# A linear-attention and Fourier-FFN kernel on one core: a form of its own for the first batch, and another plan

## The chip, the core and the metric

The kernel runs on 1 core of one Trainium2 chip. The metric is the time of one execution on the device in microseconds (us), the median of several runs; lower is better. TensorE (PE in the profile, PEld its weight loads) does the matmuls, VectorE (DVE), ScalarE (ACT) and GpSimd (POOL) the element-wise work, and DMA transfers are issued here from SyncE's queue (SP), some from ACT's and POOL's.

## The reference

```python
def _attn_ref(q, k, v, g_norm):                  # (8, 8, 576, 64) each, g_norm (64,)
    kv = np.einsum('bhsd,bhse->bhde', k, v)
    out = np.einsum('bhsd,bhde->bhse', q, kv)
    rms = np.sqrt(np.mean(out * out, axis=-1, keepdims=True) + 1e-06)
    return (out / rms * g_norm).astype(np.float32)

def _moe_ref(x, w_ch1, w_ch2):                   # x (8, 576, 512), w_ch1 (512, 2048), w_ch2 (2048, 512)
    X = np.fft.fft(x, axis=1)
    X = np.fft.fft(X, axis=2)
    u = x + np.real(X).astype(np.float32)
    mu = np.mean(u, axis=-1, keepdims=True)
    var = np.mean((u - mu) ** 2, axis=-1, keepdims=True)
    un = (u - mu) / np.sqrt(var + 1e-06)
    return (u + np.maximum(un @ w_ch1, 0.0) @ w_ch2).astype(np.float32)
```

Between the two, the attention's output is laid out as x with its 8 heads side by side (512 wide).

## The kernel before

**Stages of a batch.** Each of 8 batches passes through these steps. The k-v sums (`plan_kv`, L509): four pairs of heads, ten matmuls each, into one state kvt. The turns of q (`plan_q`, L557): a batch's 576 rows are loaded as two sides of 288, each as three classes of 96 rows (row index modulo 3), and every class of a side is transposed by four transposes, copied to fq by ACT. The attention output (`plan_out`, L582), one unit of 16 matmuls for each class t, with both sides; ACT copies it to x and squares it, DVE sums the squares (L606), POOL multiplies x by g (L617). When all three classes of a batch are summed, `plan_y` makes one scale factor for all of them (L635 to L651, ACT, POOL and DVE in turn). `plan_fold` multiplies x by it (L679), folds the two sides and the two halves of the columns (L690, then POOL's even and odd parts, L697) and splits the result into a high and a low part xh and xl (L703, L706). The sequence transform (`plan_seq`, L721) is four groups of nine matmuls, three for each class; its result is split again (L734, L738). The column transform (`plan_chn`, L755) takes six groups of six; ACT, DVE and POOL add its result to x (L767, L775, L785, L788). x is stored as u and transposed (`plan_turn`, L842) into unT, high and low (L851, L854).

**The FFN.** Per block of 512 tokens, `plan_first` (ps_h, L366) multiplies by a slice of w_ch1, 12 matmuls of 512 columns, then ReLU and split (L375, L378); `plan_second` and `plan_early` (acc, L383) multiply by the slice of w_ch2. Both use three matmuls where one would do at lower precision (high by high, high by low, low by high). The normalisation is moved behind: w_ch1's slices have their column means taken out, and a row's scale is applied at the end. A weight slice is prepared in `plan_w`: a load (raw), an ACT pass (L299), five DVE steps (L306 to L316), a sum (L896), for w_ch1 a sum over its rows (L321), a matmul with 1/512 that spreads it (ps_w, L329) and a subtraction (L333), then high and low part (L908, L913). Three slices of each are ready early (the ring wA).

**What sets the order.** Every instruction is an `Op` with an engine, a cost, a rank and what it depends on. `Plan.run` walks through time with these costs and gives each engine, whenever it is free, the ready op of lowest rank; what it emits is the engines' final order. Buffers come from rings with a fixed number each (RINGS: eight PSUM banks "p8", six k and v pieces "kv", four "fq", and so on). Rank is 10 times the batch plus a stage, FILL and more for the FFN. Where TensorE would be free, it emits filler: two matmuls of 512 columns on `still`, into a bank ps_s that nobody reads (L438). A filler op has the highest rank of all and may start from 12 us of planned time on (`SPARE_FROM`). On an engine, instructions run in that order and each waits for its semaphores. At most eight DMA transfers of the SP and ACT queues are under way: the ninth waits for the first.

## Time and profile before

| | us |
|---|---|
| median of 3 runs (lowest, highest) | 1032.32 (1023.65, 1032.94) |
| profiled execution: its own time | 1028.71 |
| profiled execution: span | 1026.9 |
| TensorE busy (98% of the span) | 1004.7 |
| DVE, ACT, POOL busy | 482.5, 328.4, 321.7 |
| mean granted clock of TensorE | 0.994 |

The page gives busy time and share of the span for each engine, the span in 40 slices, the DMA queues, the chain that ended last (89% of it on TensorE), and the costliest groups of instructions. A row of the timeline has the start in us, the duration, the engine, the line, the operation with output and inputs, how many instructions are merged in it, and in brackets how long the engine stood idle before and what ended that. A row of the windows has the stretch, its length, then busy time and number of instructions for PE, PEld, DVE, ACT and POOL, the granted clock, the share of time in which DMA engines were busy, and GB/s. A plain fp32 matmul appears as two records, a transpose or a matmul of the split kind as one. Durations of matmuls in a row overlap: a row's last one drains while the next row begins.

### The profile page before, as it was taken

What the parts mean: (1) busy time and instruction counts of PE and PEld (TensorE: products, weight loads), DVE (VectorE), ACT (ScalarE), POOL (GpSimd) and SP (SyncE); (2) the same over time, 40 slices, a digit from 0 to 9 for tenths busy, and PEclk for the clock granted to TensorE, in tenths of its full rate; (3) what the DMA queues carried; (4) which work ended last, traced back from release to release, by engine and by line L of the source; (5) the groups of instructions that cost most, each with busy time, mean ns of one, the idle gap of its engine ahead of it and who ended that gap; (6) DMA issues with size and microseconds to landing.
All of it is one profiled execution on the core that took longest, in us unless ns stands there. A gap on an engine that the chain in (4) does not pass through costs nothing.

```text
span 1026.9 us, 15221 instructions
## 1 busy us (share of the span) xinstructions
PE 1004.7 (98%) x5988; PEld 844.2 (82%) x5988; DVE 482.5 (47%) x839; ACT 328.4 (32%) x655; POOL 321.7 (31%) x332
## 2 busy tenths in 40 slices
PE   5999999999999999999999999999999999999998
PEld 4788899788888878888788888888888888888886
DVE  3778675446678657999932313131221221221312
ACT  2556665546544433343222121121021021121110
POOL 0466876655856110223253132301020020020010
PEclk9899999999999999999999999999999999999999
DMA  9998785863337653668171615230220400500201
GB/s 236 234 214 221 183 255 168 220 188 132 128 126 240 262 185 128 241 209 300 46 246 31 215 37 210 68 137 21 105 90 20 174 22 1 184 21 1 103 0 41
DMA packets 109771, 144.92 MB, mean 141 GB/s; under 512 B 51854, under 2 KB 76482, under 8 KB 104580
## 3 DMA queue, kind: packets, MB, share of 16 engines
q1 hardware_dynamic: 100980, 127.04, 39.8%
q10 hardware_dynamic: 6800, 10.62, 2.9%
q0 software_dynamic: 1920, 6.29, 2.2%
q8 instruction: 47, 0.77, 0.3%
q14 instruction: 24, 0.20, 0.1%
HBM read 92.52 MB, written 51.40 MB: 140 GB/s over the span
## 4 chain that ended last, share of the span: by engine, by line
PE 89%; DMA 3%; DVE 3%; ACT 1%; SPq 1%; issue 1%; POOL 1%; ACTq 0%; DVEq 0%; POOLq 0%
PE ps_h L366 36%; PE acc L383 36%; PE ps_f L721 3%; PE ps_f L755 3%; PE ps_o L582 3%; PE ps_k L509 2%; PE ps_s L438 2%; PE ps_t L842 1%; PE ps_q L557 1%; DMA vm<-in_v_dram 1%; DMA draw<-in_dft_s_dram 1%; DMA part_scr<-part 1%; PE ps_w L329 0%; ACT x L597 0%; DMA u_scr<-x 0%
## 5 line engine op out<-in xcount | busy, mean ns | idle before, releaser
L383 PE MATMUL acc<-w,hh 128*128 128x512 f32 x1152 | 357.5, 391 | 0.0
L366 PE MATMUL ps_h<-unTh,w 128*128 128x512 f32 x1152 | 356.0, 390 | 0.3 <-DVE pm L775 0.3
L378 DVE SCALAR_TENSOR_TENSOR hl<-ps_h,hh 128x512 fp32r<-128x512 f32 x144 | 99.3, 689 | 375.9 <-ACT hh L375 375.8
L366 PEld LDWEIGHTS ps_h<-unTh,w 128*128 128x128 f32 x1152 | 215.2, 188 | 44.7 <-PE ps_h L366 0.7
L383 PEld LDWEIGHTS acc<-w,hh 128*128 128x128 f32 x1152 | 214.0, 188 | 43.6
L375 ACT ACTIVATE hh<-ps_h 128x512 fp32r<-128x512 f32 x144 | 86.1, 598 | 474.8 <-PE ps_h L366 474.6
L383 PE MATMUL acc<-w,hl 128*128 128x512 f32 x576 | 224.6, 390 | 0.5 <-DVE hl L378 0.4
L366 PE MATMUL ps_h<-unTl,w 128*128 128x512 f32 x576 | 224.2, 389 | 0.0
L1194 POOL TENSOR_TENSOR uu<-uu,up 128x512 f32<-128x512 f32 x36 | 45.8, 1296 | 308.7 <-ACT up L1186 307.4
L383 PEld LDWEIGHTS acc<-w,hl 128*128 128x128 f32 x576 | 108.1, 188 | 23.9 <-DVE hl L378 1.3
L366 PEld LDWEIGHTS ps_h<-unTl,w 128*128 128x128 f32 x576 | 108.1, 188 | 22.6
L617 POOL TENSOR_TENSOR x<-x,gb 96x512 f32<-96x512 f32 (+1 forms) x48 | 63.4, 1337 | 56.6 <-ACT x L597 54.9
L606 DVE TENSOR_REDUCE ss<-ps_o 96x8 f32<-96x512 f32 (+1 forms) x48 | 32.9, 687 | 44.9 <-ACT ps_o L602 36.1
L913 POOL TENSOR_TENSOR w<-wap,w 128x512 fp32r<-128x512 f32 x18 | 23.3, 1293 | 96.5 <-ACT w L908 93.2
L1239 DVE SCALAR_TENSOR_TENSOR uu<-acc,rs_yb,uu 128x512 f32<-128x512 f32 x36 | 25.2, 744 | 40.6 <-PE acc L383 40.6
L697 POOL TENSOR_TENSOR xe<-ab 96x256 f32<-96x256 f32 (+1 forms) x48 | 36.7, 789 | 19.9 <-DVE ab L690 19.8
L1136 POOL TENSOR_TENSOR up<-up 128x512 f32<-128x512 f32 x16 | 20.5, 1291 | 69.2 <-DMA up<-next_scr 69.1
L721 PE MATMUL ps_f<-cs,xh 96*128 96x290 f32 (+1 forms) x192 | 40.5, 306 | 0.0
L582 PEld LDWEIGHTS ps_o<-kvt,fq 64*96 64x96 f32 (+1 forms) x768 | 34.6, 162 | 5.7 <-issue 4.2
L597 ACT COPY x<-ps_o 96x512 f32<-96x512 f32 (+1 forms) x48 | 28.1, 585 | 33.0 <-PE ps_o L582 26.4
L582 PE MATMUL ps_o<-kvt,fq 64*96 64x64 f32 (+1 forms) x768 | 37.8, 248 | 0.0
L854 DVE TENSOR_TENSOR unTl<-ps_t,unTh 128x384 fp32r<-128x384 f32 (+13 forms) x80 | 33.5, 476 | 7.9 <-ACT unTh L851 7.5
(106 smaller groups left out, 1043.2 us busy)
## 6 DMA issues: line engine op xcount, KB each, us to landing
raw<-in_moe_w_ch_dram SPq DMA_DIRECT2D x32, 512.0 KB
unTh<-unT_scr SPq DMA_DIRECT2D x11, 1024.0 KB
unTl<-unT_scr SPq DMA_DIRECT2D x11, 1024.0 KB
qt<-in_q_dram SPq DMA_DIRECT2D x16, 576.0 KB
unT_scr<-unTh SPq DMA_DIRECT2D x9, 1024.0 KB
unT_scr<-unTl SPq DMA_DIRECT2D x9, 1024.0 KB
part_scr<-part ACTq DMA_DIRECT2D x36, 256.0 KB
up<-part_scr SPq DMA_DIRECT2D x36, 256.0 KB
```

What stands on the lines that cost most here:

```text
L366: nc.tensor.matmul(ps, w[c][:, kc * P : (kc + 1) * P], unT[a][:, kc, :], start=(kc == 0 and n == 0), stop=(kc == KC - 1 and n == 2),)
L375: nc.scalar.activation(hh, ps, AF.Relu)
L378: nc.vector.scalar_tensor_tensor(hl, ps, 0.0, hh.bitcast(F32), ALU.max, ALU.subtract)
L383: nc.tensor.matmul(acc, hpair[a][:, i * P : (i + 1) * P], w[c], start=(first and n == 0), stop=(last and n == 2),)
L582: nc.tensor.matmul(pss[s].t[:n, at : at + D], fqs[side].t[half, m, :n], kvt.t[half, m], start=True, stop=True,)
L606: nc.vector.tensor_reduce(ss.t[0][:n, :, t, s::2], pss[s].t[:n].rearrange("p (u m e) -> p u m e", u=2, e=D), AX.X, ALU.add,)
L617: nc.gpsimd.tensor_tensor(v_, v_, gb[:n].unsqueeze(1).to_broadcast([n, H, D]), ALU.mult)
L697: nc.gpsimd.tensor_tensor(o[:, s], a[:, 0], a[:, 1], ALU.subtract if s else ALU.add)
L721: nc.tensor.matmul(ps.t[:, :NS], xs[t].t[a][:n, part, ch * P : (ch + 1) * P], cs[:n, part, c, t, :], start=(idx == 0), stop=(idx == 8),)
L755: nc.tensor.matmul(ps.t[:n, :ND], pt.t[a][:, part, ch, offs[t] : offs[t] + n], cd[:, part, c, ch, :], start=(idx == 0), stop=(idx == 5),)
L854: nc.vector.tensor_tensor(unTs[j].t[1][:, :, to], view()[:, :, lo:hi], unTs[j].t[0][:, :, to].bitcast(F32), ALU.subtract,)
L1194: lambda i=i: nc.gpsimd.tensor_tensor(us_[i].t, us_[i].t, parts[i].t, ALU.add),
```

## The change

It has four parts.

1. **The plan.** It first runs the first batch's ops alone (`first`, set by `mark`), notes when each starts (`aim`), and then runs all ops, in which another op may not start on an engine (or on the port that DVE and POOL share) if it would reach into the next aim by more than `SLIP`. Costs of loads are changed, TensorE's ops cost twice as much until 6.6 us of planned time, and as long as the FFN has not begun, filler goes ahead of later batches' work when TensorE's columns in the last 3414 ns are fewer than 3400. Filler may start at once. 84 filler matmuls are emitted instead of 122.
2. **Queries of batches 0 and 1** are loaded in pieces of three rows (768 bytes) instead of one row (256 bytes). A class of a head then lies apart in the tile, so `plan_q` turns it by eight plain matmuls with the identity, 64 columns of weights each, instead of four transposes.
3. **The first batch's output** (`plan_first_out`). The state is kept twice, kvt and kvg = kvt times g, and each class's output is computed with both. The first is squared and summed only, the second multiplied by the class's own scale factor straight from PSUM into x. No copy, no product with g, and no scale factor for all classes. Classes go in the order 2, 1, 0, the sequence transform is issued class by class (three matmuls to each group), and two classes' column transforms are added by DVE instead of POOL.
4. **Weights.** The first slices of w_ch1 and w_ch2 are loaded ahead of k on SP, the mean of the three early w_ch1 slices is taken by four matmuls on TensorE without the sum over rows, and their low half is made by POOL instead of DVE. The last k and v pair of batch 0 has buffers of its own.

```diff
-SPARE = 120
-SPARE_FROM = 12000
+SPARE = 200
+SPARE_FROM = 0
...
+    def w_mean4(ps, af):
+        for c in range(KC):
+            nc.tensor.matmul(
+                ps[:, :P], mean_t, af[:, c * P : (c + 1) * P], start=(c == 0), stop=(c == KC - 1)
+            )
...
+                if b == 0 and pr == NPAIR - 1:
+                    main = Buf("h", lambda c=c: h_tile(c + "h").bitcast(F32).rearrange(
+                        "p (h j d) -> p h j d", h=2, j=4
+                    ))
...
+        kvg = Buf("h", lambda: h_tile("kvg").rearrange("p (c d) -> p c d", d=D))
+        scaled = op(
+            "DVE", 330, rank(b, KV),
+            lambda: nc.vector.tensor_tensor(
+                kvg.t[:, :NPAIR].bitcast(F32), ps.t[:, : NPAIR * D].rearrange("p (c d) -> p c d", d=D),
+                gb.unsqueeze(1).to_broadcast([P, NPAIR, D]), ALU.mult,
+            ),
+            mm + [i_gb], [ps, kvg],
+        )
...
+            if wide:
+                nc.sync.dma_start(
+                    qt.t[:TR].rearrange("p (h e) -> p h e", h=H), src.rearrange("h (p j) d -> p h (j d)", j=3)
+                )
...
+                if wide:
+                    for s in range(2):
+                        at = ((2 * m + s) * 3 + j) * D
+                        nc.tensor.matmul(
+                            view()[s * D : (s + 1) * D, m, :], qt.t[:n, at : at + D], ident[:n, :n],
+                            start=True, stop=True,
+                        )
...
+    def plan_first_out(b, t, fqs, done, kvt, kvg, x, sq):
...
+        a = op("PE", 1500, r, lambda: mm(0), done, [kvt, sq] + pss[0] + fqs)
+        g = op("PE", 1500, r + 0.5, lambda: mm(1), done, [kvg, x] + pss[1] + fqs)
...
+            c = op("ACT", 594, r - D1, square, [a], [pss[0][s]])
+            reds.append(op("DVE", 684, r - D1, red, [c], [pss[0][s], sq]))
...
+        c = op("ACT", 300, r - D1, root, reds, [sq])
+        d = op("DVE", 80, r - D1, mean, reds, [sq])
+        d = op("DVE", 800, r - D1, inverse, [c, d], [sq, pss[0][0]])
...
+            ms.append(op("DVE", 690, r - D1, mul, [g, d], [pss[1][s], sq, x]))
...
-        a = op("PE", 1200, r, mm, dones + [dft["s", part]], [ps, pt] + xs)
+        if b == 0:
+            a = []
+            for t in (2, 1, 0):
+                a = [op(
+                    "PE", 400, r, lambda t=t: mm_of(t), a + [dones[t], dft["s", part]] + gate_seq,
+                    [ps, pt, xs[t]],
+                )]
...
+        quick = b == 0 and t < 2
...
+        if quick:
+            adds = [op("DVE", 720, r, lambda s=s: add_q(s), pms, [x] + pss) for s in range(2)]
...
+        early = ring_ == "wA"
+        away = slow or early and which == 1
...
-            eng = nc.gpsimd if slow else nc.vector
+            eng = nc.gpsimd if away else nc.vector
...
-                    plan_w(which, f, "wA", lambda: wA, rank(0, FOLD) + f, [], (0, 3, 11)[f])
+                    plan_w(which, f, "wA", lambda: wA, 9 + f / 10, [], (-1, 6, 9)[f])
```

**The order, at three places.** TensorE at the start of the program, before (ps_k is the k-v sums, ps_q the turns of q, ps_w the mean of a weight slice, ps_s filler):

```order
L509 MATMUL ps_k<-vm,km 64x64 x8
L509 MATMUL ps_k<-vr,kr 64x64 x2
L438 MATMUL ps_s<-still 128x512 x16
L557 MATMUL ps_q<-ident,qt 128x97 x4
L557 MATMUL ps_q<-ident,qt 128x96 x8
L329 MATMUL ps_w<-wp,mean_t 128x128
```

and after, from its first matmul to the first attention output (ps_o):

```order
L507 MATMUL ps_s<-still 128x512 x28
L393 MATMUL ps_w<-wa,mean_t 128x128 x4
L590 MATMUL ps_k<-vm,km 64x64 x8
L590 MATMUL ps_k<-vr,kr 64x64 x2
L590 MATMUL ps_k<-vh,kh 64x64 x8
L507 MATMUL ps_s<-still 128x512 x4
L660 MATMUL ps_q<-ident,qt 64x97 x8
L660 MATMUL ps_q<-ident,qt 64x96 x24
L507 MATMUL ps_s<-still 128x512 x8
L747 MATMUL ps_o<-kvt,fq 96x64 x16
L747 MATMUL ps_o<-kvg,fq 96x64 x16
```

28 filler matmuls and the first slice's mean now stand ahead of the k-v sums, and the 16 filler among the k-v sums are gone.

SP's queue at the start, before (km and kr are pieces of k, raw a weight slice, qt a side of q; gb is g, sgn_t a table of signs):

```order
L488 DMA km<-in_k_dram 128x2x256
L497 DMA kr<-in_k_dram 64x8x64
L488 DMA km<-in_k_dram 128x2x256 x2
L296 DMA raw<-in_moe_w_ch_dram 128x4x256
L296 DMA raw<-in_moe_w_ch_dram 128x1024
L424 DMA gb<-in_g_norm_dram 128x64
L532 DMA qt<-in_q_dram 96x24x64
L538 DMA qt<-in_q_dram 1x8x64
L423 DMA sgn_t<-in_sign_dram 128x18
```

and after:

```order
L493 DMA gb<-in_g_norm_dram 128x64
L359 DMA raw<-in_moe_w_ch_dram 128x4x256
L359 DMA raw<-in_moe_w_ch_dram 128x1024
L569 DMA km<-in_k_dram 128x2x256
L578 DMA kr<-in_k_dram 64x8x64
L569 DMA km<-in_k_dram 128x2x256 x2
L569 DMA kh<-in_k_dram 128x2x256
L629 DMA qt<-in_q_dram 96x8x192
L639 DMA qt<-in_q_dram 1x8x64
```

g and the two weight slices moved ahead of k; the last k piece (kh) no longer waits for a buffer of the ring, and q's rows are three times as long.

DVE around the first batch's scale factor, before (ss the sums of squares, cs and cd the transforms' tables, ab the folded result, ps_y the scale factor):

```order
L606 TENSOR_REDUCE ss<-ps_o 97x2x4 x2
L606 TENSOR_REDUCE ss<-ps_o 96x2x4
L462 TENSOR_TENSOR cd<-draw,cd 128x516 x2
L642 RECIPROCAL rs_y<-rs_s 97x48
L306 TENSOR_SCALAR ps_a<-ps_a 128x512
L651 TENSOR_TENSOR ps_y<-rs_y,rs_s 97x48
L679 TENSOR_TENSOR x<-x,ps_y 97x512 x2
L690 TENSOR_TENSOR ab<-x 97x512
```

and after, the first of the three classes:

```order
L536 TENSOR_TENSOR cs<-draw,cs 97x870 x2
L764 TENSOR_REDUCE ss<-ps_o 96x2x4 x2
L776 TENSOR_SCALAR m<-ss 96x2x8
L536 TENSOR_TENSOR cd<-draw,cd 128x516
L781 RECIPROCAL ps_o<-rs_s 96x16
L782 TENSOR_TENSOR ss<-ps_o,m 96x2x8
L783 SCALAR_TENSOR_TENSOR ss<-ss,ps_o 96x2x8
L784 SCALAR_TENSOR_TENSOR rs_s<-ss,ps_o 96x2x8
L792 TENSOR_TENSOR x<-ps_o,rs_s 96x8x64 x2
L870 TENSOR_TENSOR ab<-x 96x512
```

A class's inverse, products and fold now follow its own two sums; five of a weight slice's steps no longer stand between the reciprocal and the scale factor.

More of the change, by code (lines that the diff above doesn't have):

```diff
@@ L106, in run @@
[L106 to L126 removed]
+    def run(self):
+        first = [o for o in self.ops if o.first]
+        if first:
+            self.go(first, False)
+        for o in first:
+            o.aim = o.start
+        return self.go(self.ops, True)
@@ L443, with mark @@
     dft = {}
+    EARLY = 2
+    def mark(since):
+        for o in plan.ops[since:]:
+            o.first = True
     def plan_dft(part, dst, src, n, r, key):
@@ L673, in plan_fold @@
         r = rank(b, FOLD)
-        ms = []
-        for s in range(2):
+        given, ms = ms, list(ms or [])
+        for s in range(0 if given else 2):
             def mul(s=s):
@@ L898, in plan_w @@
             mean = bank_buf("ps_w")
-            if slow and not late_:
+            if early:
+                pass
+            elif slow and not late_:
                 e = op("POOL", 1400, r, lambda: w_sum_pool(af_(), pf_()[:, :P]), [e], held)
@@ L916, in plan_w @@
         w_done[which, f] = op(
-            "POOL" if slow else "DVE", 1291 if slow else 689, r, lo, [g], src + [tile_],
+            "POOL" if away else "DVE", 1291 if away else 689, r, lo, [g], src + [tile_],
             port=(which == 1),
```

337 lines of the change are left out of this document (241 added, 96 removed).

## Prediction

> **What bounds the kernel now.** I read the busy times first, then windows by stage, then the front row by row (start, duration, what; in brackets the idle time ahead and what ended it).
>
> ```profile
> PE 1004.7 (98%) x5988; PEld 844.2 (82%) x5988; DVE 482.5 (47%) x839; ACT 328.4 (32%) x655; POOL 321.7 (31%) x332
> L438 PE MATMUL ps_s<-still 128*128 128x512 f32 x122 | 35.3, 434 | 0.1
> 0.00:20.00 20.00, 9.58 (x78) 7.57 (x80) 5.75 (x11) 2.12 (x3) 0.90 (x8) 1.00 1.00 225
> 20.00:69.00 49.00, 46.49 (x523) 38.27 (x524) 33.63 (x47) 29.73 (x61) 24.27 (x27) 0.93 1.11 241
> 69.00:100.00 31.00, 30.29 (x379) 26.56 (x378) 27.68 (x51) 18.41 (x44) 17.91 (x21) 1.00 0.74 191
> ```
>
> TensorE is busy for 98% of the span, and from 69 us on it hardly waits: 30.29 of 31 us. Its order is fixed by the plan. So the time is the work in that order, plus the filler (ps_s, L438, whose results nobody reads), plus TensorE's waits, plus what a lowered clock adds. Only the last three can be saved, and they lie in the front: in the first 20 us TensorE is busy for 9.58 us, 5.0 of them filler.
>
> ```profile
> 1.34 0.31 DVE L430 CAST still<-ident 128x128 fp32r<-128x128 f32 x1 [0.28 <-POOL ident masks.py:199]
> 4.90 1.12 PE L509 MATMUL ps_k<-vm,km 128*64 128x64 f32 x16 [4.90 <-DMA vm<-in_v_dram]
> 8.66 0.48 PE L509 MATMUL ps_k<-vr,kr 64*64 64x64 f32 x4 [2.64 <-DMA vr<-in_v_dram]
> 9.97 1.12 PE L509 MATMUL ps_k<-vm,km 128*64 128x64 f32 x16 [0.84 <-DMA vm<-in_v_dram]
> 12.90 5.00 PE L438 MATMUL ps_s<-still 128*128 128x512 f32 x16
> 19.93 0.69 PE L509 MATMUL ps_k<-vm,km 128*64 128x64 f32 x16 [2.04 <-DMA km<-in_k_dram]
> 36.20 0.33 PE L509 MATMUL ps_k<-vr,kr 64*64 64x64 f32 x4 [1.53 <-DMA vr<-in_v_dram]
> 38.15 0.69 PE L509 MATMUL ps_k<-vm,km 128*64 128x64 f32 x16 [0.74 <-DMA vm<-in_v_dram]
> 41.30 2.16 PE L557 MATMUL ps_q<-ident,qt 97*128 97x97 f32 x12 [0.24 <-DVE cd L462]
> 43.16 3.38 PE L438 MATMUL ps_s<-still 128*128 128x512 f32 x8
> 65.25 5.21 PE ps_s L438 x22
> 70.47 4.81 PE ps_f L721 x36
> 99.17 0.73 PE L366 MATMUL ps_h<-unTh,w 128*128 128x512 f32 x2
> 131.53 1.63 PE L438 MATMUL ps_s<-still 128*128 128x512 f32 x6
> ```
>
> Waits of the first 20 us: 4.90 + 2.64 + 0.84 + 2.04 = 10.4 us. Behind them 1.53 + 0.74, and about 0.8 in small ones: 3.1. Filler: 15 stretches, the first at 12.90, the last at 131.53; from each start to the next instruction's start (the idle 2.04 taken off) they hold TensorE for 34.2 us, a little under the group's 35.3, which counts overlapped ends too. Clock: a stretch of the k-v sums takes 1.12 + 0.48 us early and 0.69 + 0.33 later; three times, 1.7 us. A second slow piece lies at 39 to 46 us:
>
> ```profile
> 34.00:36.00 2.00, 0.67 (x18) 0.53 (x16) 1.53 (x4) 1.94 (x5) 0.00 (x0) 1.00 1.19 242
> 40.00:41.00 1.00, 1.00 (x3) 0.33 (x1) 1.00 (x1) 0.64 (x1) 1.00 (x2) 0.50 1.36 210
> 46.00:47.00 1.00, 1.00 (x9) 0.82 (x8) 0.00 (x0) 0.04 (x1) 0.00 (x0) 1.00 1.10 354
> ```
>
> TensorE is busy for 0.67 of 2 us at 34, and then the granted clock is 0.50 until 46; the 12 transposes at 41.30 take 2.16 us (1.21 for 12 at 20.81, below), 0.9 more. What TensorE does not use: 10.4 + 3.1 + 34.2 + 1.7 + 0.9 = **50.3 us**.
>
> **The change, part by part.**
> *Start.* The first matmul is now filler that needs only the cast of "still" (done at 1.65), 28 of them; then the mean of the first weight, then the k-v sums. The first useful matmul thus starts at the later of two ends. Filler: 16 take 5.00 us at 12.90, while the clock comes up, so 28 take 8.8 and end at 10.5; bounds 8.3 (0.237 each, the 22 in 5.21 us at 65.25) and 13.5 (0.42 each, the 8 in 3.38 us at 43.16). Weight: its load now stands ahead of k on SP's queue.
>
> ```profile
> 0.00:10.00 10.00, 1.62 (x22) 1.34 (x22) 0.57 (x4) 1.49 (x2) 0.90 (x8) 1.00 0.79 220
> 9.90:12.90 3.00, 2.93 (x41) 2.49 (x41) 0.00 (x0) 0.03 (x1) 0.00 (x0) 1.00 1.10 356
> 14.00:15.00 1.00, 1.00 (x4) 0.81 (x3) 0.93 (x2) 0.00 (x0) 0.00 (x0) 1.00 1.41 143
> 12.87 0.63 ACT L299 ACTIVATE ps_a<-raw 128x512 f32<-128x512 f32 x1 [10.64 <-DMA raw<-in_moe_w_ch_dram]
> 13.53 0.70 DVE L306 TENSOR_SCALAR ps_a<-ps_a 128x512 f32<-128x512 f32 x1 [11.88 <-ACT ps_a L299]
> 17.18 0.69 DVE L896 TENSOR_TENSOR wa<-ps_a,wp 128x512 f32<-128x512 f32 x1
> ```
>
> The first 10 us brought 2.2 MB, by estimate hardly any before 2 us. The weight with g is 0.55 MB, and as much of v comes beside it from ACT's queue: 1.1 MB, landed at about 6.2 us. ACT's 0.63 and six DVE steps (13.53 to 17.87) follow: 11.2, with handovers **11.8**. Bounds 10.5 (the filler's end) and 15.3 (weight as late as 10 us). The four k-v sums follow; they need 3.46 MB (two weights, k, v), which at the 356 GB/s of 9.90 to 12.90 are in by about 13.5, so loads do not hold them.
>
> *Query pieces.* At 14 to 15 us, with 256-byte query pieces under way, the queues moved 143 GB/s; with longer ones 356. For 768 bytes no row exists. I take 290, nearer the upper row, as three short pieces become one: batch 0's 1.18 MB end at 17.6; bounds 16.9 and 21.8. TensorE comes to the turn that needs the last of it at about 19, so 1.4 us of lateness is hidden.
>
> *Added work on TensorE.* Turning q for batches 0 and 1 takes 8 plain matmuls (16 records) instead of 4 transposes, 12 times.
>
> ```profile
> 20.81 1.21 PE L557 MATMUL ps_q<-ident,qt 97*128 97x97 f32 x12
> 31.11 2.95 PE L582 MATMUL ps_o<-kvt,fq 64*96 64x64 f32 x64
> ```
>
> Three old turns are 1.21 us with their last drain, so 0.37 each. A plain record costs 0.046 (64 in 2.95 us) or, in the k-v sums, 0.043 (16 in 0.69). I take 0.046, whose weights are the like 96 columns: 0.74 a turn, +0.37 twelve times is 4.4 (bounds 3.8, and 13 at the 0.092 of an old turn's record). Second states: three more ps_o of 32 records, 1.5 each, 4.5. The mean as four matmuls instead of one, for three weights: six more records of about 0.046, +0.3 each, 0.8. Together **9.7 us**.
>
> *Filler left.* 84 matmuls instead of 122: 28 stand at the start, 56 at 0.237 are **13.3**.
>
> *Chain of the first batch.* Before, all three classes waited for the last one's sums: the scale factor came at 47.55, the last xl at 68.0, the first sequence transform at 70.3. Now each class goes by itself, on DVE, ACT and POOL. It costs TensorE only where it ends after TensorE gets there.
>
> ```profile
> 47.55 0.22 DVE L651 TENSOR_TENSOR ps_y<-rs_y,rs_s 97x48 f32<-97x48 f32 x1 [2.44 <-ACT fq L561]
> 28.82 0.57 ACT L602 ACTIVATE ps_o<-ps_o 96x512 f32<-96x512 f32 x1
> 31.19 0.93 ACT L459 ACTIVATE cs<-draw 97x870 fp32r<-97x870 f32 x1 [1.01 <-DMA draw<-in_dft_s_dram]
> L606 DVE TENSOR_REDUCE ss<-ps_o 96x8 f32<-96x512 f32 (+1 forms) x48 | 32.9, 687 | 44.9 <-ACT ps_o L602 36.1
> 49.12 0.69 DVE L690 TENSOR_TENSOR ab<-x 97x512 f32<-97x512 f32 x1
> 49.96 1.43 POOL L697 TENSOR_TENSOR xe<-ab 97x256 f32<-97x256 f32 x2 [6.03 <-DVE ab L690]
> 57.92 2.00 DVE L690 TENSOR_TENSOR ab<-x 96x512 f32<-96x512 f32 x2
> 65.47 2.54 POOL L706 TENSOR_TENSOR xl<-xe,xh 96x512 fp32r<-96x512 f32 x2 [0.36 <-ACT xh L703]
> L345 DVE RECIPROCAL rs_yb<-rs_sb 128x4 f32<-128x4 f32 x9 | 1.6, 178 | 2.4 <-ACT rs_sb L340 2.4
> L347 DVE TENSOR_TENSOR rs_tb<-rs_yb,bm 128x4 f32<-128x4 f32 x9 | 2.2, 243 | 0.3
> ```
>
> TensorE: 11.8, the mean 0.6, four k-v sums 3.5, filler 0.9, four turns 3.0, filler 1.9: first ps_o at 21.7. Then six ps_o 9.0, batch 1's four k-v sums 3.5, six turns 4.4, ten filler 2.4, 24 sequence matmuls of the first two classes (36 in 4.81 us) 3.2, one mean 0.6: it reaches the third class's at **45**. Chain: on ACT the two copies of cs (0.93 each) stand ahead of the first squares; their load ends near 22.8 us (1.7 MB behind q, at 340 GB/s), so DVE's first sum starts at about 25.3. DVE then has six sums and six products (0.69, the products as the fold), three folds (0.69), three inverses of four tiny steps (0.18 to 0.24 by L345 and L347, 0.75), cd's two halves (1.3) and the means: 14.2, to 39.5. POOL is at the second class's xl until about 40.2; 1.43 for the even and odd parts, ACT 0.6 and 1.27 for xl end at **43.6**. Chain and TensorE so arrive within 1.4 us of each other, and the first ps_h comes near 67 instead of 99.17, with 14 us of k-v sums, turns and ps_o left for later.
>
> *Costed at nothing.* POOL gets the low half of w1 and loses the products with g, ACT loses the copies of ps_o; both have room (24.27 and 29.73 of 49 us). DVE gets the quick adds of two classes and loses the sums over w and the low halves. With 27.68 of 31 us at 69 to 100 its cover is thin: each us it is late shows. SP issues as many transfers as before.
>
> **Sum.** Before 50.3; after 11.8 + 13.3 = 25.1; freed 25.2; added 9.7; net 15.5. New waits: behind 20 us the front of before, planned as well, shows 3.1 us of waits, 0.9 of half clock on work and about 2.5 on filler at 39 to 46, 6.5 in all. All of it could come again or none (bounds 0 and 9, as 1.4 us of slack stands where 22 filler stood); I take 5. Gain 10.5. The profiled execution took 1028.7 us (span 1026.9), 3.6 under the median of 1032.3 and above the lowest, 1023.7. 1028.7 - 10.5 = **1018 us**.
>
> **Rivals.**
> *Late chain, most of the gain given back.* With q at 143 GB/s (4.2 us later), or with DVE and POOL in each other's way (the folds of two classes at 57.92 took 2.00 us, not 1.38), what exceeds 1.4 us shows ahead of the third class: 3 to 6 us more, to 1024. For it: little slack, and ACT goes in order with cs ahead of the squares. Against: three engines of the chain have idle time behind 20 us. Chance 0.28.
> *Fewer waits.* What the front of before shows does not come back: 1013. Chance 0.17.
> *The clock falls (the other side).* It fell to 0.50 for 7 us behind the sparse 34 to 38. Here a gap of 1.3 us stands between the start's filler and the mean; the 2.04 us at 17.9 left the clock whole. If the weight lands 3 us later the gap is 4.3, and the front's small matmuls may then run at half clock until dense work returns; 12 transposes lost 0.9 of 2.16 us. At that rate 25 us at half clock eat the gain, and 50, nearly the whole front to 67, give 1039. Chance 0.05. [...]
> *The start's filler warms nothing.* Then it ends at 13.5 and k-v runs cold, 1.7 + 1.7: 1021, part of the forecast's range.
> *Nothing gained.* Later loads hold TensorE and the front's gain is lost: 1028. For it: DMA stands at 1.11 until 69 us. Against: two batches of short pieces less. Chance 0.08.
>
> **How the numbers follow.** Forecast, 1014 to 1021: 0.42; the others as above. Over 1% is 10.3 us, about what a measurement of this kernel can tell. Faster by it (1018.4 or less): 0.17 and 0.33 of the forecast, 0.50. Slower: 0.05. Within: 0.45. The range 1010 to 1027 leaves out the clock, most of "nothing gained" and a little below 1010, 0.15 to 0.2.
>
> **What would show it.** Right: first filler near 1.7 us, the mean at 11 to 13, ps_o near 22, sequence transforms near 40, first ps_h at 65 to 70, turns of 0.74 us, no clock of 0.50 behind 10 us. Wrong: k-v sums that wait for DMA behind 14 us, ps_f for POOL's xl, ps_h for DVE's unTl, or a mean (ps_w) held at 75 to 85 us by the third weight's steps on DVE.

## The result, and the profile after

The changed kernel takes 1019.69 us in the median of 20 runs (1016.76 to 1028.97), the kernel before, run beside it, 1028.07 (20 runs, 1023.65 to 1033.94). The ratio on record, which is not that of the two medians, is 0.9928, with a 95% interval of 0.9907 to 0.9949: 0.7% faster, inside the predicted range, and inside the 1% that the prediction called about the limit of what can be told. The profiled executions are 1028.71 and 1019.38 us, 9.3 apart, spans 1026.9 and 1017.6; the prediction said 10.5 less. The size is right, but the terms behind it are partly others, and some of them cancel by luck.

The busy times of the changed kernel, and the filler's group (busy, mean ns of one, idle time ahead):

```profile
PE 1005.8 (99%) x6208; PEld 846.9 (83%) x6208; DVE 474.4 (47%) x855; ACT 325.6 (32%) x651; POOL 311.6 (31%) x320
L507 PE MATMUL ps_s<-still 128*128 128x512 f32 x84 | 25.6, 443 | 1.6 <-DVE still L499 1.6
```

This gives a ledger that every profile here can be put through: span less PE busy is TensorE's idle time, PE busy less the filler's busy time is its work. Before: 22.2 idle, 35.3 filler, 969.4 work. After: 11.8, 25.6, 980.2. Idle time and filler fall by 20.1 us, work grows by 10.8.

Its windows, in the stretches that were shown of before:

```profile
0.00:20.00 20.00, 14.68 (x96) 11.91 (x96) 5.35 (x11) 3.26 (x5) 2.11 (x8) 0.80 0.90 234
20.00:69.00 49.00, 48.38 (x717) 42.42 (x714) 36.74 (x76) 25.37 (x55) 15.26 (x17) 0.94 0.82 208
69.00:100.00 31.00, 30.17 (x359) 25.04 (x358) 25.89 (x45) 21.33 (x48) 18.37 (x24) 1.00 1.04 268
```

TensorE is busy for 14.68 instead of 9.58 us of the first 20 (8.4 of it are filler), and for 48.38 instead of 46.49 up to 69. Two more windows each, of the kernel before and then of the changed one, show what the prediction had not looked at:

```profile
135.00:300.00 165.00, 162.85 (x1461) 143.55 (x1460) 96.73 (x181) 93.95 (x214) 104.24 (x118) 0.99 0.58 181
300.00:500.00 200.00, 197.54 (x958) 164.79 (x957) 160.95 (x251) 75.96 (x144) 58.45 (x56) 1.00 0.59 207
```

```profile
135.00:300.00 165.00, 164.79 (x1477) 145.42 (x1476) 102.52 (x193) 93.66 (x214) 108.26 (x122) 1.00 0.57 180
300.00:500.00 200.00, 199.29 (x949) 165.91 (x948) 156.31 (x246) 76.37 (x143) 54.01 (x51) 1.00 0.59 205
```

Behind 135 us, where the change alters the order of the work and not the work of a batch, 4.61 us of idle time became 0.92. The kernel before also loses clock there. The first number behind the engines' busy times is the granted clock:

```profile
206.36:209.77 3.41, 3.41 (x16) 3.41 (x16) 0.71 (x2) 0.80 (x2) 0.09 (x1) 0.50 0.02 5
```

It follows two waits of 0.64 and 0.56 us for POOL's xl. A group of three ps_f matmuls takes 0.40 us just ahead of it; five groups here take 3.53 us, so about 1.5 us are lost. The changed kernel has no such stretch.

The front row by row, changed kernel:

```profile
1.64 8.40 PE L507 MATMUL ps_s<-still 128*128 128x512 f32 x28 [1.64 <-DVE still L499]
8.59 0.62 ACT L362 ACTIVATE ps_a<-raw 128x512 f32<-128x512 f32 x1 [6.36 <-DMA raw<-in_moe_w_ch_dram]
13.73 2.05 PE L393 MATMUL ps_w<-wa,mean_t 128*128 128x128 f32 x8 [3.69 <-DVE wa L1109]
15.71 1.12 PE L590 MATMUL ps_k<-vm,km 128*64 128x64 f32 x16
23.55 3.96 PE L660 MATMUL ps_q<-ident,qt 97*64 97x97 f32 x64
29.48 1.57 PE L747 MATMUL ps_o<-kvt,fq 64*96 64x64 f32 x32
48.78 0.53 PE L913 MATMUL ps_f<-cs,xh 96*128 96x290 f32 x2
54.57 0.52 PE L913 MATMUL ps_f<-cs,xh 97*128 97x290 f32 x2
75.97 0.71 PE L435 MATMUL ps_h<-unTh,w 128*128 128x512 f32 x2
```

The filler starts and ends as forecast (1.64 to 10.04). The first weight does not land at 6.2 but just ahead of ACT's step at 8.59; so the mean waits until 13.73, and between filler and mean TensorE is idle for 3.69 us. What that gap did is read from three windows that are cut where the granted clock changes (the clock stands in the same place as above):

```profile
8.79:12.20 3.41, 1.25 (x6) 0.71 (x4) 2.82 (x5) 0.42 (x1) 0.00 (x0) 1.00 1.11 301
12.20:25.85 13.65, 12.12 (x120) 10.15 (x122) 6.05 (x10) 2.01 (x4) 1.27 (x1) 0.50 1.09 270
25.85:29.26 3.41, 3.41 (x48) 2.90 (x44) 1.18 (x3) 2.65 (x6) 0.00 (x0) 1.00 0.95 216
```

For 13.65 us TensorE ran at half clock, although from 13.73 on it was never idle. The k-v sums took 1.12 + 0.48 us each instead of 0.69 + 0.33, and the first ps_o came at 29.48 instead of about 22; 4.2 us of that are the clock's, as e1_cover will show. This is the mechanism of the rival "the clock falls", to which the prediction gave 0.05.

The runs show it too. The mean clock was 0.998 in one of the 20 runs (1016.8 us), 0.992 to 0.995 in twelve (1017.9 to 1021.5), 0.988 in five (1023.2 to 1025.0) and 0.985 in two (1028.9 and 1029.0). The slow end of this kernel's spread goes with the time that it spends at half clock; within the twelve the two do not go together.

### The profile page after: what moved, and what is told of

Read it like the earlier page. It is cut to its first block, busy times and chain, and to the rows that moved or that the text cites. A ratio compares the mean times of both kernels' runs of the same rounds, so it can differ in the third digit from the quotient of the medians.

```text
span 1017.6 us, 15655 instructions
## 1 busy us (share of the span) xinstructions
PE 1005.8 (99%) x6208; PEld 846.9 (83%) x6208; DVE 474.4 (47%) x855; ACT 325.6 (32%) x651; POOL 311.6 (31%) x320
## 4 chain that ended last, share of the span: by engine, by line
PE 90%; DMA 5%; DVE 3%; ACT 1%; issue 1%; ACTq 0%; SPq 0%; DVEq 0%
PE ps_h L435 37%; PE acc L452 36%; PE ps_o L691 3%; PE ps_f L955 3%; PE ps_f L901 3%; PE ps_k L590 3%; DMA vm<-in_v_dram 2%; DMA part_scr<-part 2%; PE ps_t L1053 1%; PE ps_q L666 1%; PE ps_s L507 1%; DMA raw<-in_moe_w_ch_dram 1%; PE ps_q L660 1%; DMA km<-in_k_dram 1%; PE ps_f L913 0%
## 5 line engine op out<-in xcount | busy, mean ns | idle before, releaser
L452 PEld LDWEIGHTS acc<-w,hh 128*128 128x128 f32 x1152 | 213.9, 188 | 43.6
L726 POOL TENSOR_TENSOR x<-x,gb 96x512 f32<-96x512 f32 (+1 forms) x42 | 54.5, 1316 | 53.2 <-ACT x L706 50.5
L715 DVE TENSOR_REDUCE ss<-ps_o 96x8 f32<-96x512 f32 (+1 forms) x42 | 28.8, 687 | 34.8 <-ACT ps_o L711 29.4
L1065 DVE TENSOR_TENSOR unTl<-ps_t,unTh 128x384 fp32r<-128x384 f32 (+14 forms) x80 | 33.4, 481 | 8.0 <-ACT unTh L1062 8.0
L955 PE MATMUL ps_f<-cd,pt 128*96 128x258 f32 (+1 forms) x288 | 35.9, 282 | 0.0
L955 PEld LDWEIGHTS ps_f<-cd,pt 128*96 128x96 f32 (+1 forms) x288 | 34.8, 162 | 0.7
L901 PE MATMUL ps_f<-cs,xh 97*128 97x290 f32 (+1 forms) x168 | 34.3, 299 | 0.0
L691 PEld LDWEIGHTS ps_o<-kvt,fq 64*96 64x96 f32 (+1 forms) x672 | 30.7, 162 | 4.2 <-issue 3.2
## 6 DMA issues: line engine op xcount, KB each, us to landing
unTh<-unT_scr SPq DMA_DIRECT2D x11, 1024.0 KB
unTl<-unT_scr SPq DMA_DIRECT2D x11, 1024.0 KB
unT_scr<-unTh SPq DMA_DIRECT2D x9, 1024.0 KB
unT_scr<-unTl SPq DMA_DIRECT2D x9, 1024.0 KB
```

The lines of the kernel that those rows point to most:

```text
L452: nc.tensor.matmul(acc, hpair[a][:, i * P : (i + 1) * P], w[c], start=(first and n == 0), stop=(last and n == 2),)
L691: nc.tensor.matmul(pss[s].t[:n, at : at + D], fqs[side].t[half, m, :n], kvt.t[half, m], start=True, stop=True,)
L726: nc.gpsimd.tensor_tensor(v_, v_, gb[:n].unsqueeze(1).to_broadcast([n, H, D]), ALU.mult)
L901: nc.tensor.matmul(ps.t[:, :NS], xs[t].t[a][:n, part, ch * P : (ch + 1) * P], cs[:n, part, c, t, :], start=(idx == 0), stop=(idx == 8),)
L955: nc.tensor.matmul(ps.t[:n, :ND], pt.t[a][:, part, ch, offs[t] : offs[t] + n], cd[:, part, c, ch, :], start=(idx == 0), stop=(idx == 5),)
L1065: nc.vector.tensor_tensor(unTs[j].t[1][:, :, to], view()[:, :, lo:hi], unTs[j].t[0][:, :, to].bitcast(F32), ALU.subtract,)
```

## The experiments

All kernels were timed beside the kernel before. "Idle", "filler" and "work" are the ledger of the profiled span, in us. (In e6_dense, 5.0 us of the work are its 14 added filler matmuls.) The medians come from different rounds: the kernel before had medians of 1028.1 to 1029.6 in them. The ratios compare with the kernel before in the same rounds.

| kernel | median of runs (lowest) | ratio to before, 95% | span | clock | idle | filler | work |
|---|---|---|---|---|---|---|---|
| before | 1028.1 (1023.7) | | 1026.9 | 0.994 | 22.2 | 35.3 | 969.4 |
| changed | 1019.7 (1016.8) | 0.9907 to 0.9949 | 1017.6 | 0.992 | 11.8 | 25.6 | 980.2 |
| e1_cover | 1026.2 (1020.7) | 0.9944 to 0.9996 | 1023.9 | 0.988 | 9.9 | 30.6 | 983.4 |
| e2_w2_behind_k | 1024.0 (1017.5) | 0.9937 to 0.9998 | 1016.9 | 0.994 | 10.9 | 26.8 | 979.2 |
| e3_q256 | 1026.7 (1022.4) | 0.9950 to 0.9988 | 1023.1 | 0.994 | 12.7 | 36.8 | 973.6 |
| e4_costs | 1026.8 (1020.3) | 0.9950 to 0.9992 | 1023.4 | 0.998 | 19.5 | 36.2 | 967.7 |
| e5_cover_both | 1021.7 (1015.0) | 0.9902 to 0.9957 | 1014.1 | 1.000 | 7.6 | 31.6 | 974.9 |
| e6_dense | 1019.4 (1016.4) | 0.9872 to 0.9959 | 1016.1 | 0.998 | 11.5 | 24.5 | 980.1 |
| e7_form | 1021.1 (1017.6) | 0.9919 to 0.9959 | 1015.8 | 0.993 | 11.4 | 30.1 | 974.3 |
| e8_start | 1029.3 (1024.8) | 0.9971 to 1.0013 | 1027.9 | 0.994 | 18.3 | 26.5 | 983.1 |
| e9_form_cover | 1019.3 (1018.9) | 0.9889 to 0.9942 | 1017.2 | 0.996 | 10.9 | 33.8 | 972.5 |
| e10_start_alone | 1035.1 (1033.9) | 1.0043 to 1.0093 | 1034.2 | 0.991 | 13.6 | 49.7 | 970.9 |
| e11_nocols | 1025.5 (1022.6) | 0.9951 to 0.9995 | 1024.3 | 0.988 | 16.6 | 21.6 | 986.1 |
| e12_cover_three | 1019.4 (1017.3) | 0.9897 to 0.9951 | 1017.2 | 1.000 | 9.2 | 33.1 | 974.9 |

### The gap and the clock

**e1_cover** fills the gap of 3.69 us.

```diff
+MORE = 16
...
-                for _ in range(0 if pools else 2):
+                calls.append(1)
+                more = MORE if len(calls) == 14 else 0
+                for _ in range(0 if pools else 2 + more):
                     nc.tensor.matmul(ps.t, still, wide, start=True, stop=True)
```

> The changed kernel with 16 more filler matmuls ahead of the first mean (44 instead of 28), nothing else moved. They fill the 3.69 us in which TensorE waited for the first weight (10.04 to 13.73), 16 x 0.237 = 3.8 us. Theory (the gap halves the clock, and half clock costs time): no granted clock of 0.50 between 12 and 26 us, the mean at 13.7 to 14.0 as before, first ps_o at 25 to 26 instead of 29.48, time 1014 to 1016 against 1019.7 of the changed kernel, ratio to the kernel before 0.986 to 0.989, and the runs lie closer together. Rival (what half clock costs is taken up by later waits anyway): clock whole, but TensorE then waits for loads or for the first batch's chain between 25 and 60 us, 1018 to 1020. Second rival (the clock does not depend on the gap): 0.50 from 12 us again, 1019 to 1020.

The gap went, the clock stayed whole behind it, and the first ps_o came at 25.28 us: as the theory said. But the kernel is slower than the changed one (ratio 0.9970 against 0.9928, intervals that just touch), and its 1026.2 us lie beyond the ranges of the theory and of both rivals. Its windows between the changes of the clock, and the row at 32.93:

```profile
29.71:33.12 3.41, 0.82 (x22) 0.64 (x20) 2.94 (x6) 3.41 (x7) 0.00 (x0) 1.00 1.07 245
33.12:57.02 23.90, 23.65 (x248) 19.67 (x246) 16.18 (x34) 5.68 (x15) 7.23 (x8) 0.50 0.68 169
57.02:60.43 3.41, 3.41 (x26) 3.26 (x24) 0.46 (x1) 1.01 (x2) 1.73 (x3) 1.00 0.82 252
```

```profile
32.93 0.99 PE L594 MATMUL ps_k<-vm,km 128*64 128x64 f32 x16 [2.59 <-DVE ss L768]
```

TensorE now reaches batch 1's k-v sum 2.6 us before DVE's sums release a PSUM bank. What holds the sums is a load: ACT and DVE prepare the table cs first in their order, and ACT waits for it.

```profile
28.16 0.93 ACT L537 ACTIVATE cs<-draw 97x870 fp32r<-97x870 f32 x1 [3.13 <-DMA draw<-in_dft_s_dram]
```

So the sums start at 31.60, hardly earlier than the 31.90 of the changed kernel, although the first ps_o is 4.2 us earlier. The hole again halves the clock, this time for 23.90 us, in which TensorE is busy for 23.65. So the first rival was right about the place (the work ahead is hidden by a wait for the chain) and the theory about the first fall; neither had a second fall. In the changed kernel the half clock of the first 26 us had delayed TensorE by 4.2 us, more than this wait.

**e6_dense** asks what brings the clock back: 14 filler matmuls of 512 columns behind the mean.

```diff
             def go(pr=pr, ts=ts):
+                for _ in range(14 if b == 0 and pr == 0 else 0):
+                    nc.tensor.matmul(ps.t, still, still.unsqueeze(1).to_broadcast([P, KC, P]), start=True, stop=True)
```

> The changed kernel with 14 filler matmuls of 512 columns (into the bank of the k-v sums, before these begin) between the first mean and the first k-v sum; the gap of 3.7 us ahead of the mean stays. Theory (dense work brings the clock back, k-v sums do not): the clock falls near 12 us as before, but is whole by 23 us at the latest instead of 25.85, the k-v sums take 0.69 + 0.33 us instead of 1.12 + 0.48 where it is back; 14 filler cost 4 to 6 us and 3 to 5 us come back, so 1018 to 1022. Rival (half clock lasts a set time, or any busy 3.4 us end it): whole at 25 to 26 us again, or already behind the mean; then 1022 to 1025, or 1023 to 1025.

```profile
8.25:11.66 3.41, 1.54 (x7) 0.94 (x5) 2.43 (x4) 0.62 (x1) 0.00 (x0) 1.00 1.10 314
11.66:15.08 3.42, 1.47 (x11) 1.42 (x12) 2.04 (x4) 0.00 (x0) 0.00 (x0) 1.00 0.98 284
15.08:18.49 3.41, 3.41 (x10) 2.64 (x9) 0.38 (x1) 1.15 (x2) 1.28 (x1) 0.50 1.09 249
18.49:30.00 11.51, 11.51 (x185) 9.32 (x185) 6.00 (x10) 4.49 (x9) 0.00 (x0) 1.00 1.09 249
```

```profile
14.49 5.04 PE L586 MATMUL ps_k<-still 128*128 128x512 f32 x14
19.46 0.69 PE L592 MATMUL ps_k<-vm,km 128*64 128x64 f32 x16
```

The idle time (3.82 us) lies in the first two windows; half clock follows the second, and one window full of 512-column matmuls ends it: 3.41 us instead of 13.65. The k-v sums behind it take 0.69 + 0.33. The time is that of the changed kernel (median 1019.4): 5.0 us of filler pay for themselves, no more.

**e5_cover_both** fills both holes: e1_cover's 16, and 11 ahead of the wide turns at 28 us (`MORE = {14: 16, 21: 11}`, by the count of the filler op).

> The kernel of e1_cover (16 more filler in the gap before the first mean) with 11 more filler matmuls ahead of batch 1's first wide turns, as long as the 2.6 us in which e1_cover's TensorE waited for DVE's sums at 30.35 us. Theory (a stretch of 3.41 us with too few columns halves the clock, and at half clock k-v sums and ps_o, with 64 columns a record, cannot bring it back): with both holes filled there is no granted clock of 0.50 between 6 and 100 us, and the 24 us at half clock of e1_cover's profile go; 1016 to 1018, most runs within 3 us of each other and at a clock of 0.995 or more. Rival (the clock falls for another reason): 0.50 again behind 30 us, 1022 to 1028. Second rival (the filler only pushes the chain of the first batch back): clock whole, waits for DVE or POOL at 35 to 50 us, 1019 to 1022.

In the profile the clock is whole from 6.7 us to the end, and the span, 1014.1 us, is the shortest of all. Five of 11 runs are like it (clock 0.999 or 1.000, 1015.0 to 1016.8 us); the other six have 0.990 to 0.997 and 1021.7 to 1027.3. The theory holds for the profile and five runs; the median, 1021.7, is no better than the changed kernel's. Its work is 974.9 us, the changed kernel's 980.2: by this half clock costs that kernel 5.3 us of work.

**e12_cover_three** thickens the thinnest stretch that is left (`MORE = {14: 16, 21: 11, 24: 5}`).

> The kernel of e5_cover_both with 5 more filler matmuls (7 instead of 2) at 42.5 us, ahead of the k-v sum for which TensorE waited 1.06 us at 43.3 us; by its profile's rows the thinnest 3.41 us of that kernel lie there, from 40.5 to 46 us, with about 3100 to 3500 columns where most stretches hold 4500 to 7400. Five of e5_cover_both's 11 runs had a clock of 0.999 or 1.000 and took 1015.0 to 1016.8, the other six 0.997 down to 0.990 and 1021.7 to 1027.3. Theory (those six fell in the thin stretch, by where the grid of clock windows lay in them): at least two thirds of the runs at 0.998 or more, median 1015 to 1017.5, ratio to the kernel before 0.986 to 0.989, faster than both kernels. Rival (they fell elsewhere, or the filler pushes the chain): again about half of the runs below 0.998, median 1019 to 1022.

The clock was 0.998 or more in five of 8 runs: under the theory's two thirds, and 8 runs cannot tell it from five of 11. Those five took 1017.3 to 1019.8 us, and the median, 1019.4, is that of the rival. The work is again 974.9; idle time and filler are 3.1 us more, as the span is. The row that the filler was meant to cover, in e5_cover_both and then here:

```profile
44.35 0.69 PE L593 MATMUL ps_k<-vm,km 128*64 128x64 f32 x16 [1.06 <-DMA vm<-in_v_dram]
```

```profile
47.14 0.69 PE L593 MATMUL ps_k<-vm,km 128*64 128x64 f32 x16 [1.04 <-DMA vm<-in_v_dram]
```

The k-v sum comes 2.8 us later and still waits for v, 1.04 us. The load did not come at a set time; it moved with TensorE. That it waits for a buffer that TensorE's earlier sums release is the likely reason, and was not tried.

**e11_nocols** takes the plan's column count away (`FULL = 3400` becomes 0).

> The changed kernel with the plan's column count off (no filler ahead of later batches' work); everything else stays, and the plan is made anew, with 72 filler matmuls instead of 84. Theory (stretches of k-v sums and ps_o alone hold too few columns and let the clock fall or keep it low): 12 filler fewer save at most 2.9 us, but half clock lasts longer than 13.65 us in the profile, mean clock 0.990 or lower in many runs, 1019 to 1026. Rival (busy time is what counts, and this filler is waste): 1015 to 1018, with no more half clock than before.

```profile
13.05:23.29 10.24, 9.60 (x92) 7.85 (x92) 2.81 (x5) 1.52 (x3) 1.27 (x1) 0.50 1.07 264
40.36:43.77 3.41, 2.29 (x47) 2.02 (x47) 2.88 (x9) 0.60 (x2) 1.42 (x3) 1.00 1.12 230
43.77:57.43 13.66, 12.89 (x111) 12.32 (x112) 7.00 (x8) 3.53 (x8) 4.79 (x6) 0.50 0.70 177
```

A second fall, at 43.77, keeps TensorE at half clock for 13.66 more us; the work rises to 986.1 us. 12 filler matmuls fewer cost 5.8 us in the median (4.6 by the ratios), as the theory had it: the plan's count pays here.

### The start

**e2_w2_behind_k** moves only the load of w_ch2's first slice behind k.

```diff
-        nc.sync.dma_start(flat, w_source(which, f))
+        if (which, f) == (2, 0):
+            later.append(lambda: nc.sync.dma_start(flat, w_source(which, f)))
+        else:
+            nc.sync.dma_start(flat, w_source(which, f))
...
+                    if last:
+                        later.pop()()
```

> The changed kernel with the load of the first slice of w_ch2 issued behind the last k piece of batch 0 instead of ahead of k; TensorE's order is the same. Theory (the first slice of w_ch1 landed at 8.4 us instead of 6.2 because w_ch2's slice shared the queues with it): its ACT step starts at 6.5 to 7.2, the mean at 11.6 to 12.3, so the gap behind the 28 filler is 1.6 to 2.3 us, the clock stays whole, and the time falls by the 1.5 to 2 us of earlier start and some 3 to 5 of half clock, to 1013 to 1016. Rival (the load is late for its own latency, not for what stands beside it): ACT's step at 8.3 or later, gap 3.5 us, clock 0.50, 1019 to 1020. Second rival (w_ch2's slice comes too late): clock whole, but DVE's chain of the first batch is pushed back and TensorE waits at 45 to 60 us, 1016 to 1020.

```profile
8.44 0.63 ACT L367 ACTIVATE ps_a<-raw 128x512 f32<-128x512 f32 x1 [6.21 <-DMA raw<-in_moe_w_ch_dram]
```

ACT's step comes at 8.44 instead of 8.59: w_ch2's slice is not what makes the weight late. The theory fell; the first rival has the step and the clock right, but not the gap or the time. In this profile the filler ended at 11.18, its 28 matmuls taking 9.54 us instead of 8.40, the gap was 2.40 us, and the clock still fell, from 14.63 to 24.87. Only three of its 12 runs had a clock above 0.990 (1017.5 to 1018.7); the median is 1024.0. Here k moves up into the freed place, so this run alone cannot tell whether the weight is held by its own latency. e10_start_alone, below, can.

**e8_start** undoes most of the start: k ahead of the weights, no filler before 12 us. g stays at the head of SP's queue.

```diff
-SPARE_FROM = 0
+SPARE_FROM = 12000
...
-                    plan_w(which, f, "wA", lambda: wA, 9 + f / 10, [], (-1, 6, 9)[f])
+                    plan_w(which, f, "wA", lambda: wA, 9 + f / 10, [], (0, 6, 9)[f])
```

> The changed kernel with the start of before: k ahead of the first weights on SP, and no filler before 12 us of planned time; the rest of the change stays, and the plan is made anew. Theory (the new start gains nothing: 13.7 us before the first useful matmul and half clock behind it against 10.4 us of waits and 5 us of filler before): first ps_o at 25 to 29 us, 1016 to 1021. Rival (filler and weights first are worth what the prediction put on them, 10.4 + 5.0 + 1.7 against 11.8, so 5 us): 1022 to 1026.

```profile
0.00:20.00 20.00, 9.81 (x90) 8.06 (x91) 3.14 (x9) 2.39 (x4) 0.84 (x7) 1.00 0.92 224
20.00:69.00 49.00, 46.58 (x651) 40.87 (x650) 33.55 (x62) 21.71 (x47) 13.71 (x16) 0.90 0.86 196
```

```profile
7.58 1.12 PE L590 MATMUL ps_k<-vm,km 128*64 128x64 f32 x16 [7.58 <-DMA km<-in_k_dram]
```

The whole gain is gone: 1029.3 us, more than even the rival's 1022 to 1026. First ps_o is earlier (27.32), but idle time is 18.3 us instead of 11.8, and TensorE also waits behind 20 us. The first k-v sum waits for k until 7.58; in the kernel before, whose queue begins with k, it came at 4.90. So this is not quite the start of before, and up to 2.7 us of the idle time may come of that. Five of its runs had a clock of 0.999 or 1.000 and still took 1024.8 to 1026.7, so the clock is not the whole reason. The weight's DVE steps, which the start puts into DVE's idle first 16 us, now come behind 16 us, and the third class's transform starts at 60.48 instead of 54.57. This fits the theory of DVE's early steps, but the plan was made anew, so other orders changed with it.

**e10_start_alone** puts the start into the kernel of e4_costs (below): `SPARE_FROM = 0`, `SPARE = 200`, first weights loaded first.

> The kernel of e4_costs (before, with the load figures of the change in the plan) with the new start alone: the first weights loaded ahead of k, filler from the start on and up to 200 of it as the plan wants; 256-byte pieces, no form, no aims, no column count. Theory (the start's gain, 9 us in e8_start, comes from DVE's early weight steps and stands by itself): 1015 to 1019 against 1026.8 of e4_costs. Rival (the start pays only together with the longer query pieces, which let the loads of 1 MB of weights ahead of k through): TensorE fills or waits longer for k and q, 1024 to 1032.

1035.1 us, 6.5 slower than before: 178 filler matmuls and a first sequence transform at 73.93. The theory fell, and the time went beyond even the rival's range. Alone, the start is a loss, though one wait of 3.81 us for a copy of fq, from 144.5 to 148.3, is part of it.

This run answers what e2_w2_behind_k left open. The same weight is loaded first, with w_ch2's slice behind it; but g comes later on SP's queue (issued at 7.27). The first 3 us of the changed kernel, and then of this one with ACT's first step on the weight:

```profile
0.00:3.00 3.00, 1.36 (x3) 1.16 (x4) 0.50 (x4) 1.49 (x2) 0.84 (x7) 1.00 0.08 18
```

```profile
0.00:3.00 3.00, 1.29 (x3) 1.10 (x4) 0.57 (x4) 1.49 (x2) 0.91 (x8) 1.00 0.30 67
6.14 0.63 ACT L299 ACTIVATE ps_a<-raw 128x512 f32<-128x512 f32 x1 [3.90 <-DMA vm<-in_v_dram]
```

The queues move 67 GB/s instead of 18, and the weight is in by 6.14 us (the row names v, whose loads ACT was issuing until then, so the weight may have been in earlier). So its own latency is not what holds it in the changed kernel. What stands ahead of it there is g, only 32 KB, but 128 pieces of 256 bytes; e8_start, with g ahead of k, moves 15 GB/s in its first 3 us, the kernel before 78. This points to g's load at the head of the queue. No run moves g alone.

### Query pieces, form and plan

**e3_q256** sets `EARLY = 0`: pieces of 256 bytes, transposes.

> The changed kernel with the queries of batches 0 and 1 in 256-byte pieces and turned by transposes, as before the change; the plan is made anew by its own rules. Theory (768-byte pieces only buy loads that arrive earlier, and the loads are not what holds TensorE): 12 turns of 0.37 instead of 0.74 us save 4.4 us, less what waits on loads come back (0 to 4): 1015 to 1020. Rival (the short pieces' 143 GB/s holds the first batch): batch 0's queries land some 4 us later, TensorE waits ahead of the turns or fills, 1022 to 1027.

1026.7: the rival's number, but not all at its place. The work falls by 6.6 us (4.4 by estimate are the turns, the rest less half clock: 3.41 us near 14 and 6.83 from 188, instead of 13.65). But 126 filler matmuls stand where 84 stood, 11.2 us more of filler. 22 of the 42 stand around batch 0's turns, and yet the first ps_o comes at 29.02, level with the 29.48 of the changed kernel. The time is lost behind 30 us, with 22 more filler matmuls, 1.5 us more of waits and that second stretch at half clock. TensorE's extra 4.4 us were the cheaper side.

**e7_form** takes the first batch's own form away and keeps the rest.

```diff
+FORM = False
...
-            if b == 0:
+            if b == 0 and FORM:
                 muls[t] = plan_first_out(
...
-        quick = b == 0 and t < 2
+        quick = b == 0 and t < 2 and FORM
...
-        if b == 0:
+        if b == 0 and FORM:
             a = []
```

> The changed kernel without the first batch's own form: one state, one scale factor for all three classes, sequence transform at once, POOL's adds as in the other batches; the start, the 768-byte pieces and the plan's rules stay, and the plan is made anew. Theory (the form carries the gain: the sequence transform starts at 48.8 us instead of 70.3): it starts at 60 to 70 us again, TensorE fills or waits 8 to 14 us more, of which the 4.5 us of second states come off, 1022 to 1028. Rival (the second states cost what the earlier transform brings): 1017 to 1021.

```profile
65.90 0.43 PE L902 MATMUL ps_f<-cs,xh 97*128 97x290 f32 x2
90.66 0.71 PE L436 MATMUL ps_h<-unTh,w 128*128 128x512 f32 x2
```

The sequence transform is back at 65.90 and the first ps_h at 90.66, 17 and 15 us later than in the changed kernel, and yet the time is 1021.1, with an interval that overlaps the changed kernel's; the profiled span is even 1.8 us shorter at nearly the same clock (0.993 and 0.992). 14 more filler matmuls (4.5 us) are as much as the second states cost. The rival holds. That later batches' k-v sums, turns and ps_o fill TensorE just as well fits this; it was not counted.

**e9_form_cover** is e7_form with e1_cover's 16 filler matmuls.

> The kernel of e7_form (the change without the first batch's own form) with 16 more filler ahead of the first mean, as in e1_cover. e7_form's profile had 13.65 us at half clock behind the gap, and no wait for the first batch's chain near 30 us. Theory (the form buys little, half clock costs some 5 us where no chain hides it): no 0.50 between 6 and 100 us, 1011 to 1014, faster than the changed kernel (1019.7) and than e5_cover_both's whole-clock runs (1015 to 1017). Rival (the half clock hides behind loads here too, as in e1_cover): a new hole behind 20 us and a clock of 0.50 there, 1017 to 1023.

```profile
33.55 0.33 PE L594 MATMUL ps_k<-vr,kr 64*64 64x64 f32 x4 [1.48 <-DMA vr<-in_v_dram]
```

1019.3, above the theory's 1014 and the rival's case: loads now make the hole (1.48 us for vr), and the clock falls from 35.56 to 42.39. Its six runs lie within 1.6 us, but none is faster than the changed kernel's better ones.

**e4_costs** is the kernel before with three numbers of the plan changed.

```diff
-    LAND = 1900
-    ISSUE = 120
+    LAND = 2200
+    ISSUE = 450
...
-    def dma(self, kb, rank, emit, after=(), bufs=(), eng="SP", rate=340):
+    def dma(self, kb, rank, emit, after=(), bufs=(), eng="SP", rate=345):
```

> The kernel before with only the plan's three figures for loads changed as in the change (landing 2200, issue 450, rate 345); nothing else. Behind 69 us the kernel before waited for 4.6 us and the changed one for 0.9, which the prediction did not foresee. Theory (these waits go because the plan now knows loads better and gives them another order): waits behind 69 us of 0 to 2 us and 1023 to 1026. Rival (they go because the front is 9 us shorter and the batches stand differently): 4 to 5 us of waits again, 1027 to 1030.

1026.8, ratio 0.9971, 0.8 us above the theory's range. In the stretches of 135 to 300 and 300 to 500 us, where the 4.6 us stand, it idles for 1.77 us instead of 4.61. So in this plan the load figures alone take away 2.8 of the 3.7 us. They are no sure remedy: e10_start_alone has the same figures and idles there for 5.30 us, 3.81 of it in the wait named above.

No version beats both kernels by more than its interval. e5_cover_both has the lowest runs, e6_dense, e9_form_cover and e12_cover_three have medians within 0.4 us of the changed kernel.

## Why the prediction was right, and where it was not

The sum, in us, on the side of what TensorE does not use plus what is added:

| | predicted | measured |
|---|---|---|
| before: unused in the front | 50.3 | 50.3 |
| before: waits behind 135 us | left as they are | 4.6 |
| before: half clock at 206 us | not seen | 1.5 |
| after: until the first useful matmul | 11.8 | 13.7 |
| after: filler behind it (56) | 13.3 | 15.9 |
| after: waits behind 20 us, and half clock on work | 5 | 2.4 + 5.3 |
| added work | 9.7 | 9.8 |
| gain | 10.5 | 9.3 |

The filler is taken from each stretch's start to the next instruction's; the added work is what the span leaves over, and the rows agree with its price (four turns 2.80 us at whole clock in e6_dense, so 0.70 each; 32 records of ps_o 1.5).

*Start.* The filler's end was right. The step that failed is the weight at "about 6.2 us": it is in near 8.4, and the first 5 us carry 111 GB/s. The rate was taken from a queue that begins with k; for a weight at the head of the queue 6.2 is right (6.14 in e10_start_alone). g, ahead of it here, was counted by its 32 KB. The upper bound of the prediction, 15.3, held.

*Clock.* The condition was nearly right ("if the weight lands 3 us later": it was 2.2, and the gap 3.69), and its chance of 0.05 was the largest error: it happened in the profile, and by their clocks in nearly every run. The size was also off: 13.65 us at half clock, not 25, worth 5.3 us. Two readings failed. The prediction put the fall at a gap of 4.3 us; 3.69 brought it here, and e1_cover's hole of 2.6 us and e2_w2_behind_k's of 2.40 were enough. And its gap is one of idle time alone: in the 3.42 us ahead of the fall at 39.11, in the kernel before, TensorE was busy for 2.17.

```profile
35.69:39.11 3.42, 2.17 (x45) 1.79 (x45) 2.33 (x4) 3.36 (x8) 2.62 (x3) 1.00 1.17 167
```

Half clock was to last "until dense work returns": in e1_cover it went on through 23.90 us, 23.65 of them busy, with k-v sums, ps_o and turns; in e6_dense one step of 512-column filler, 3.41 us, ended it.

*Query pieces.* 290 GB/s was assumed for 768 bytes. At 16 to 18 us, when hardly anything else was under way, the queues moved less, 232; with TensorE late itself, no turn waited for it.

```profile
16.00:18.00 2.00, 2.00 (x36) 1.76 (x32) 0.50 (x1) 1.16 (x2) 0.68 (x1) 0.50 1.09 232
```

The price on TensorE was right. That they are worth more than they cost was not said; e3_q256 shows 7.0 us by the medians, 4.2 by the ratios.

*Chain of the first batch.* This step named DVE's chain as what TensorE arrives with, and the earlier ps_h as what follows. Both came some 9 us late: the first sum at 31.90 instead of 25.3, the third class's xl at 52.94 instead of 43.6, TensorE at 54.57 instead of 45. So the chain never held TensorE there, by 1.6 us, close to the 1.4 of the forecast, and by luck. The load of cs, put at 22.8, is the term that was too small; in e1_cover ACT waits for it until 28.16, and there the chain does hold TensorE. And the earlier ps_h (75.97, from 99.17) is worth nothing measurable: e7_form gives it up for 1.4 us by the medians, with overlapping intervals. The form was not the part that carries the change.

*Costed at nothing.* Right for the changed kernel: its TensorE waits for no step of POOL, and for DVE's weights behind the start only 0.2 us.

*New waits, 5 us.* Half clock took that place and a little more; waits proper were 2.4, of which 1.4 for v of later batches.

*What was not in the sum.* The prediction said of the time from 69 us on that TensorE "hardly waits", from a window that ends at 100; the 4.6 us behind 135 and the half clock at 206 were left as they are. Their going paid for the late weight and the clock. e4_costs gets most of the 4.6 by the plan's load figures, e10_start_alone with the same figures does not; why this plan is free of them stays open. The total came out right by luck, as these errors cancel: 1.9 + 2.6 + 2.7 too little for the front, and 4.6 + 1.5 not foreseen. Of the signs that were to show the prediction right, the first filler (1.64) and, at whole clock, the turns (0.70) came; the mean, ps_o, the sequence transforms and ps_h all came later than said, and the clock fell. Of the signs that were to show it wrong, one came in small: k-v sums waited 1.4 us for v.

*Which part carries the gain.* Undone singly, the start costs 9.6 us, the pieces 7.0, the column count 5.8, the form 1.4; together 23.8, against a gain of 8.4. By the ratios it is 6.6, 4.2, 4.6 and 1.1, against 7.4. Either way they are not a sum, and each run has a plan of its own, so a figure holds for a part and the plan made without it. The start needs other parts: alone it loses 6.5 (e10_start_alone).
